# Products of 32 columns behind the first units' stages, and the global normalising step placed behind the next unit's maxima

## The chip, the cores and the metric

The kernel runs on one core of one Trainium2 chip. The metric is the device time of one execution in microseconds. PE is the engine of matrix products (TensorE), with its weight loads shown apart as PEld; DVE is VectorE, ACT is ScalarE, POOL is GpSimd, and SP (SyncE) issues the DMAs.

## The reference

The reference computes attention over 8 batches of 8 heads with 512 local and 32 global positions, head dimension 64, and then a gated feed-forward network on the result. A global query attends to all 544 keys. A local query attends to the 32 global keys and to the local keys at a distance of at most 32.

```python
k_all = np.concatenate([k_g, k_l], axis=2)
v_all = np.concatenate([v_g, v_l], axis=2)
out_g = sm(scale * q_g @ k_all.T) @ v_all            # sm: softmax over the keys, + 1e-9 in the sum
s_ll  = np.where(abs(i - j) <= 32, scale * q_l @ k_l.T, -1e9)
out_l = sm(concat([scale * q_l @ k_g.T, s_ll])) @ v_all
x     = concat([out_g, out_l])   # 4608 tokens of 512
gate  = 1 / (1 + exp(-(x @ w_gate)))                 # 512 x 1536
out   = (gate * (x @ w_val)) @ w_out                 # 1536 x 512
```

All is in 32-bit floats.

## The kernel before, in words

**Two streams in one.** The feed-forward network (`ffn_stream`) is the backbone of the program. It goes through the tokens in chunks: the two halves of batch 0 (256 tokens each), batches 1 to 7 (512 each), and at the end all global tokens. For each chunk it goes through 12 tiles of 128 of the 1536 inner columns. Each step is 12 products of the gate (PSUM tile `bank_g`, L400), 12 of the value (`bank_v`, L400) and 12 of the output of the step before (`bank_o`, L437). Each operand is split into a high and a low part and the product is made of three passes over them, which is why there are 12 products for 4 slices of the contraction.

After every 4 products the stream yields, and a clock `now` goes on by one slot. A batch of 512 tokens thus has 12 x 9 = 108 slots. The attention of the next chunk is cut into events with due times on this clock (`att_events`), and after each yield all events that are due are written into the program.

**A unit of attention** (`local_unit`) takes two blocks of 128 queries of one head through four stages, due 0, 3, 6 and 9 slots after the unit's start (`STAGES`). Units start 4 slots apart.

- Stage 0: scores on PE (L234, into `bank_x`), then for each block the masked maxima on VectorE (L248, into `nm`, with the scores copied to `s_sb`) and the exponentials on ScalarE (L251).
- Stage 1: sum and reciprocal (L254, L255) and the normalising products (L260, into `p_buf`), on VectorE.
- Stage 2: transposes on PE (L268), a copy on ScalarE and, for the high and low split, a subtraction on VectorE (L279, L280, into `pt`).
- Stage 3: products with the values on PE (L300, into `bank_x`), a copy on ScalarE (L302), a sum on VectorE (L303) and one on POOL (L304).

**The global group.** After the two units of a head its 32 global queries are scored (L313 to L318) and copied into a quarter of `pg_buf` (L320, L321). After the 4th and the 8th head, the group of four heads goes through `global_group`: maxima (L328) and exponentials (L330); the normalising step on VectorE (L335, 128 x 544); five transposes on PE (L340) with their copies (L344) and low parts (L346, into `ptg`); and 20 products (L361). Its stages are due at 0, 3, 6 and 9 slots (`GSTAGES`). After the first group of a batch, the next unit starts 4 slots after the group; after the second group the next unit belongs to the next chunk. There are 16 groups, three of them "native": in the first chunks, operands are taken as plain floats without a split.

**PSUM.** `bank_g`, `bank_v`, and all `bank_x` and `bank_y` tiles share four buffers (tag `att`). The four `bank_o` accumulators have the rest.

**What sets the order.** Each engine works through its own queue in order. The order in a queue is made by a planner when the program is built: it goes by readiness in its own reckoning of durations, and of what is ready takes first what was written first. `with tc.issue_after(ins)` adds an edge: what is issued inside on the engine of `ins` comes behind `ins` in that engine's queue. Three anchors are kept for this: `anchor[0]` is the last L248 that was written, `exp_at[0]` the last L251, `low_at[0]` the last L280.

**The filling products.** `fill(n)` multiplies the identity by itself into a PSUM bank that nobody reads (L117). Eight calls come before the first unit. In the first chunk (8 units, `first`) one call follows the scores, one the transposes and one the products of each unit: 24 calls. The products wait for nothing but the identity.

Of the kernel before, what the change touches and what calls it, by code (L numbers as in the profile page):

```python
# [17 lines left out]
P = 128  # L18
D = 64
SL = 512  # L20
SG = 32
# [22 lines left out]

BASE, PER = 3, 4
STAGES = (0, 3, 6, 9)
GSTAGES = (0, 3, 6, 9)
LOAD_QK, LOAD_V, SPLIT_QK, SPLIT_V = 16, 9, 10, 4
LOAD_V_NATIVE = 4

# [2 lines left out]
FILL = (8, 1)  # L53
# [12 lines left out]
def kernel(ctx, tc, qk, v, w_gate, w_val, w_out, out_l, out_g):  # L66
    nc = tc.nc
# [15 lines left out]
    ident = const.tile([P, P], F32, name="ident")  # L83
# [4 lines left out]
    for c0, nc0, lo, hi in ((0, 128, 0, 64), (160, 64, 128, -64)):  # L88
        cols = mid[:, c0:c0 + nc0]
# [22 lines left out]

    fill_ps = ps.tile([P, DM], F32, name="bank_o3")

    def fill(n):
        for i in range(n):
            nc.tensor.matmul(fill_ps[:, 0:P], ident, ident, start=True, stop=True)  # L117

    fill(FILL[0])
    conv_bufs = []  # L120
    anchor, exp_at, low_at = [None], [None], [None]
# [102 lines left out]
    def local_unit(T, blocks, x32s, h, b0):  # L224
        ks, k0s, q0 = T["qk"], T["k0"], T["q0"]
        nat = T["native"]
# [6 lines left out]
                js = slice(k0 + j * BLK + w0, k0 + j * BLK + w1)  # L233
                nc.tensor.matmul(s_ps[:, i, w0:w1], qj, kt[:, js], start=t == 0, stop=t == last)  # L234
        if T["first"]:
            fill(FILL[1])
        if T["first"]:
            s_sb = ffn.tile([P, 2, WIN], F32, name="s_first", tag="ob", bufs=2)
        else:
# [27 lines left out]
        for t, (_, c) in enumerate(tiles):  # L267
            nc.tensor.transpose(pt_ps[:, t], pb[:, c:c + P], ident)  # L268
        if T["first"]:
            fill(FILL[1])  # L270
        if nat:
            if T["first"] and h % 2:
                pt = ffn.tile([P, 4, P], F32, name="pt_first", tag="th", bufs=1)[:, 0:nt]
# [14 lines left out]
        if nat:  # L288
            o_ps = ps.tile([64, 2, P], F32, name="bank_x", tag="att", bufs=4)
            for i, j in enumerate(blocks):  # L290
                for n, tl in enumerate(KEYS[j]):
                    nc.tensor.matmul(o_ps[:, i], vt[:, tl, :], pt[:, at[tl]], start=n == 0, stop=n == 1)  # L292
            if T["first"]:
                fill(FILL[1])
            nc.scalar.copy(dst, o_ps)
            return
        o_ps = ps.tile([P, 2, 2, P], F32, name="bank_x", tag="att", bufs=4)
# [25 lines left out]
    def global_group(Ts, b, g):  # L323

        nat = Ts[0]["native"]
        mg = small.tile([P, 4], F32, name="mg")
        p = pg[:, G0:G0 + KALL]
        nc.vector.tensor_reduce(mg[:, 0:1], p, axis=AX.X, op=ALU.max)  # L328
        nc.vector.tensor_scalar(mg[:, 1:2], mg[:, 0:1], -0.125, None, op0=ALU.mult)
        nc.scalar.activation(p, p, AF.Exp, bias=mg[:, 1:2], scale=0.125, accum_out=mg[:, 2:3])  # L330
        nc.vector.tensor_scalar_add(mg[:, 3:4], mg[:, 2:3], 1e-9)
        nc.vector.reciprocal(mg[:, 3:4], mg[:, 3:4])
        yield
        with tc.issue_after(low_at[0].ins) if not nat else nullcontext():
            nc.vector.tensor_scalar(p, p, mg[:, 3:4], None, op0=ALU.mult)  # L335
        yield
        banks = [ps.tile([P, n, GH, SG], F32, name="bank_y", tag="att", bufs=4) for n in (4, 1)]
        for j in range(5):
            o = banks[j // 4][:, j % 4].rearrange("p r q -> p (r q)")
            nc.tensor.transpose(o, pg[:, j * P:(j + 1) * P], ident)  # L340
        pt = att.tile([P, 5, GH, 2, SG], F32 if nat else F32R, name="ptg_nat" if nat else "ptg", tag="ptg", bufs=1)
        for bank, t in zip(banks, (pt[:, 0:4], pt[:, 4:5])):
            hi, lo = t[:, :, :, 0], t[:, :, :, 1]
            nc.scalar.copy(hi, bank)  # L344
            if not nat:
                nc.vector.tensor_tensor(lo, bank, hi.bitcast(F32), op=ALU.subtract)  # L346
        yield
        g0 = b * SG
        xg = xgq[g0 // P][g0 % P:g0 % P + SG, g * GH * D:(g + 1) * GH * D].rearrange("q (r d) -> q r d", d=D)
        if nat:  # L350
            o_ps = ps.tile([SG, GH, D], F32, name="bank_x", tag="att", bufs=4)
            for r, T in enumerate(Ts):
                for j in range(5):
                    nc.tensor.matmul(o_ps[:, r], pt[:, j, r, 0], T["v"][:, V_GLOBAL[j], :], start=j == 0,
                                     stop=j == 4)
            nc.scalar.copy(xg, o_ps)
            return
        o_ps = ps.tile([2 * SG, GH, 2 * D], F32, name="bank_x", tag="att", bufs=4)
        for r, T in enumerate(Ts):
            for j in range(5):  # L360
                nc.tensor.matmul(o_ps[:, r], pt[:, j, r].rearrange("p c q -> p (c q)"), T["v"][:, V_GLOBAL[j], :],  # L361
                                 start=j == 0, stop=j == 4)
        y = att.tile([SG, GH, 2 * D], F32, name="yq", tag="t0", bufs=1)
        nc.scalar.copy(y, o_ps[SG:2 * SG])
        nc.vector.tensor_tensor(y, o_ps[0:SG], y, op=ALU.add)
        nc.gpsimd.tensor_tensor(xg, y[:, :, 0:D], y[:, :, D:2 * D], op=ALU.add)
# [82 lines left out]
    def att_events(ci, start, per, tail=0):  # L449
# [21 lines left out]
        def adv(h, i):  # L471
            if (h, i) not in gens:
                gens[h, i] = (local_unit(heads[h], units[i], x32s, h, blocks[0]) if i < nu
                              else global_group(heads[h + 1 - GH:h + 1], b, h // GH))
            next(gens[h, i], None)

        npu = nu + (1 if with_g else 0)
        for h in range(NH):
# [7 lines left out]
            for i in range(npu):  # L486
                t0 = base + per * i
                if i == nu:
                    ev.append((t0, 2, lambda T=T, h=h: global_scores(T, h % GH)))
                    if h % GH < GH - 1:  # L490
                        continue
                for o in STAGES if i < nu else GSTAGES:
                    ev.append((t0 + sc * o, 2, lambda h=h, i=i: adv(h, i)))
# [122 lines left out]
```

## Time and profile before

| what | value |
|---|---|
| median of 3 runs | 1168.41 us (1167.89 to 1168.96) |
| the profiled execution | 1169.24 us |
| its span, first to last instruction | 1167.2 us |
| PE busy | 1142.7 us, 98% |
| ScalarE busy | 748.2 us, 64% |
| VectorE busy | 723.9 us, 62% |
| POOL busy | 365.4 us, 31% |
| mean granted TensorE clock | 1.000 |

A row of the profile gives a line of the kernel, an engine, an operation with its tiles, a count, the busy time, the mean duration of one in nanoseconds, and the idle time of the engine before it with what ended it. A row of the timeline begins with the start in microseconds from the span's start and the duration. Ends of PE's products are modelled, and products overlap in the pipeline, so a busy PE is not PE at its peak. A row of the stretches gives busy time and number of instructions for PE, PEld, DVE, ACT and POOL, then the granted clock, the share of the DMA engines and GB/s.

### The profile page before, as it was taken

To read this page: it belongs to the slowest core of one execution; us is meant where nothing else is said; L and a number is where in the kernel's file an instruction comes from. 1 tells how busy PE (TensorE), PEld (TensorE's weight loads), DVE (VectorE), ACT (ScalarE), POOL (GpSimd) and SP (SyncE) were. 2 spreads that over 40 slices of the span, in tenths; PEclk is the share of its full clock that TensorE was granted. 3 is DMA by queue.
4 is the path that set the end of the run, shared out by engine and by line. 5 is a ranking of instruction groups with operands and counts; after the bars stand their busy time and mean duration, and the time that the engine had idled before them with its cause. 6 is when DMAs were issued, how large, how long until landed. Compare 5 with 4: busy or idle time off the path is not lost.

```text
span 1167.2 us, 18885 instructions
## 1 busy us (share of the span) xinstructions
PE 1142.7 (98%) x6596; PEld 958.7 (82%) x6596; DVE 723.9 (62%) x1950; ACT 748.2 (64%) x1700; POOL 365.4 (31%) x372
## 2 busy tenths in 40 slices
PE   8999999999999999999999999999999999999998
PEld 7777888888888888888888888887888888888897
DVE  5888746566676666656676666666666666533343
ACT  5888767666676676666676676677675676432343
POOL 1000135234452444334452444344442443100000
PEclk9999999999999999999999999999999999999999
DMA  8898744343333333443343333353243332122143
GB/s 299 289 297 295 237 135 129 96 123 101 104 117 119 106 112 99 109 143 100 102 117 119 108 110 99 109 151 109 84 127 121 109 106 75 55 90 72 55 157 115
DMA packets 59486, 151.79 MB, mean 130 GB/s; under 512 B 6144, under 2 KB 19456, under 8 KB 59392
## 3 DMA queue, kind: packets, MB, share of 16 engines
q1 hardware_dynamic: 59392, 150.59, 42.6%
q8 instruction: 52, 0.85, 0.3%
q14 instruction: 42, 0.34, 0.1%
HBM read 135.36 MB, written 15.20 MB: 129 GB/s over the span
## 4 chain that ended last, share of the span: by engine, by line
PE 74%; ACT 11%; DVE 10%; issue 2%; DMA 1%; POOL 1%; SPq 0%; DVEq 0%; ACTq 0%
PE bank_g L400 19%; PE bank_o L437 19%; PE bank_v L400 18%; PE bank_x L234 4%; PE bank_y L268 3%; PE bank_x L300 3%; ACT s_sb L251 3%; PE bank_x L292 2%; DVE p_buf L260 2%; DVE pt L280 1%; PE bank_x L361 1%; DVE bank_v L421 1%; DVE t L303 1%; DVE bank_v L420 1%; ACT mn L414 1%
## 5 line engine op out<-in xcount | busy, mean ns | idle before, releaser
L400 PE MATMUL bank_v<-xt,wv 128*128 128x512 f32 (+1 forms) x1440 | 328.2, 364 | 6.8 <-DVE t L303 6.8
L400 PE MATMUL bank_g<-xt,wg 128*128 128x512 f32 (+1 forms) x1440 | 329.7, 364 | 0.2 <-DVE t L303 0.2
L437 PE MATMUL bank_o<-wo,hh 128*128 128x512 f32 x1224 | 325.6, 398 | 0.6 <-ACT hh L423 0.6
L400 PEld LDWEIGHTS bank_v<-xt,wv 128*128 128x128 f32 x1440 | 237.2, 189 | 43.7 <-DVE t L303 8.3
L400 PEld LDWEIGHTS bank_g<-xt,wg 128*128 128x128 f32 x1440 | 236.9, 189 | 37.1 <-issue 2.9
L437 PEld LDWEIGHTS bank_o<-wo,hh 128*128 128x128 f32 x1224 | 217.1, 188 | 40.5 <-ACT hh L423 1.4
L251 ACT ACTIVATE s_sb<-s_sb,nm 128x192 f32<-128x192 f32 (+1 forms) x240 | 110.7, 462 | 92.0 <-DVE nm L248 91.7
L205 POOL TENSOR_TENSOR kl<-qk_raw,qk_hi 128x704 fp32r<-128x704 f32 x52 | 88.6, 1704 | 156.8 <-ACT qk_hi L204 151.6
L423 ACT CAST hh<-bank_v 128x512 fp32r<-128x512 f32 (+1 forms) x120 | 62.7, 522 | 109.9 <-DVE bank_v L421 109.1
L218 POOL TENSOR_TENSOR vhl<-v_raw,vhl 128x512 fp32r<-128x512 f32 x52 | 67.3, 1294 | 186.5 <-ACT vhl L217 85.4
L303 DVE TENSOR_TENSOR t<-bank_x,t 64x512 f32<-64x512 f32 x104 | 70.8, 681 | 86.5 <-ACT t L302 85.4
L408 ACT ACTIVATE th<-bank_g 128x512 f32<-128x512 f32 (+1 forms) x120 | 63.9, 532 | 90.4 <-PE bank_g L400 89.8
L304 POOL TENSOR_TENSOR x<-t 64x256 f32<-64x256 f32 x104 | 76.9, 740 | 124.0 <-DVE t L303 101.2
L413 DVE TENSOR_SCALAR mn<-bank_g 128x512 f32<-128x512 f32 (+1 forms) x108 | 67.7, 627 | 76.8 <-ACT th L408 76.7
L248 DVE CUSTOM_DVE_ANT_0 s_sb<-bank_x,masks 128x192 f32<-128x192 f32 (+1 forms) x240 | 80.8, 370 | 30.7 <-PE bank_x L234 27.1
L420 DVE TENSOR_TENSOR bank_v<-bank_v,mn 128x512 f32<-128x512 f32 (+1 forms) x120 | 73.7, 614 | 42.1 <-PE bank_v L400 36.8
L424 DVE TENSOR_TENSOR hh<-bank_v,hh 128x512 fp32r<-128x512 f32 (+1 forms) x120 | 73.2, 610 | 41.0 <-ACT hh L423 40.2
L373 POOL TENSOR_TENSOR xt<-x,xt 128x512 fp32r<-128x512 f32 (+1 forms) x36 | 42.7, 1187 | 152.7 <-ACT xt L372 108.2
L280 DVE TENSOR_TENSOR pt<-bank_y,pt 128x384 fp32r<-128x384 f32 x104 | 64.6, 621 | 37.7 <-ACT pt L279 37.0
L260 DVE TENSOR_SCALAR p_buf<-s_sb,r 128x192 f32<-128x192 f32 (+1 forms) x240 | 83.0, 374 | 2.0
L207 POOL TENSOR_TENSOR qk_hi<-qk_raw,qk_hi 64x256 fp32r<-64x256 f32 x104 | 78.6, 776 | 4.1
L300 PEld LDWEIGHTS bank_x<-pt,vhl 128*128 128x128 f32 x416 | 61.6, 189 | 18.7 <-issue 7.5
(108 smaller groups left out, 1577.1 us busy)
## 6 DMA issues: line engine op xcount, KB each, us to landing
wo<-wo_dram SPq DMA_DIRECT2D x116, 512.0 KB, 3.5
qk_raw<-in_qk_dram SPq DMA_DIRECT2D x104, 312.0 KB, 4.4
v_raw<-in_v_dram SPq DMA_DIRECT2D x52, 256.0 KB, 2.6
out_dram<-ob SPq DMA_DIRECT2D x34, 256.0 KB, 2.9
xt<-in_w_gate_dram SPq DMA_DIRECT2D x12, 512.0 KB, 6.1
xt<-in_w_val_dram SPq DMA_DIRECT2D x12, 512.0 KB, 6.2
xt<-in_w_out_dram SPq DMA_DIRECT2D x12, 512.0 KB, 5.9
v_nat<-in_v_dram SPq DMA_DIRECT2D x8, 512.0 KB, 6.5
```

The costliest lines, as they stand in the source:

```text
L205: nc.gpsimd.tensor_tensor(kl, t[:, K0:Q1], hi[:, K0:Q1].bitcast(F32), op=ALU.subtract)
L207: nc.gpsimd.tensor_tensor(hi[64:128, r], t[64:128, r], hi[64:128, r].bitcast(F32), op=ALU.subtract)
L248: anchor[0] = nc.vector.tensor_tensor_reduce(out=s_sb[:, i, w], in0=s_ps[:, i, w], in1=mid[:, w], scale=-0.125, scalar=3.0e38, op0=ALU.add ...
L251: exp_at[0] = nc.scalar.activation(s_sb[:, i, w], s_sb[:, i, w], AF.Exp, bias=nm[:, i:i + 1], scale=-1.0, accum_out=sm[:, i:i + 1])
L260: nc.vector.tensor_scalar(pb[:, places[i] + w0:places[i] + w1], s_sb[:, i, w0:w1], r[:, i:i + 1], None, op0=ALU.mult)
L280: low_at[0] = nc.vector.tensor_tensor(pt[:, 1], pt_ps, pt[:, 0].bitcast(F32), op=ALU.subtract)
L300: nc.tensor.matmul(o_ps[:, i], vt[:, tl, :], pt[:, :, at[tl], :], start=n == 0, stop=n == 1)
L303: nc.vector.tensor_tensor(t0, o_ps[0:64], t0, op=ALU.add)
L304: nc.gpsimd.tensor_tensor(dst, t0[:, :, 0], t0[:, :, 1], op=ALU.add)
L400: nc.tensor.matmul(acc, w[a][:, t, fs], xt[:, c, t, x0:x0 + ntok], start=n == 0, stop=n == 11)
L420: nc.vector.tensor_tensor(acc, acc, mn, op=ALU.mult)
L437: nc.tensor.matmul(o_ps[t], ph[:, a, t * P:(t + 1) * P], pwo[:, c], start=f2 == 0 and i == 0, stop=f2 == NF - 1 and i == 2)
```

## The change

The 24 calls of `fill` behind the stages of the first units multiply the identity by its first 32 columns instead of all 128; the eight calls ahead of them stay. The global group's second stage (the normalising step L335) is due 5 slots after its start instead of 3, the third (transposes) 7 instead of 6. In the groups that are not native, the step's edge goes to the last maxima written, `anchor[0]`, instead of the last low part of a transposed unit, `low_at[0]`. As the next unit's stage 0 is due 4 slots after a first group's start, its two L248 are written by then.

```diff
-GSTAGES = (0, 3, 6, 9)
+GSTAGES = (0, 5, 7, 9)
...
-    def fill(n):
+    def fill(n, cols=P):
         for i in range(n):
-            nc.tensor.matmul(fill_ps[:, 0:P], ident, ident, start=True, stop=True)
+            nc.tensor.matmul(fill_ps[:, 0:cols], ident, ident[:, 0:cols], start=True, stop=True)
...
         if T["first"]:
-            fill(FILL[1])
+            fill(FILL[1], SG)
...
         if T["first"]:
-            fill(FILL[1])
+            fill(FILL[1], SG)
...
             if T["first"]:
-                fill(FILL[1])
+                fill(FILL[1], SG)
...
-        with tc.issue_after(low_at[0].ins) if not nat else nullcontext():
+        with tc.issue_after(anchor[0].ins) if not nat else nullcontext():
             nc.vector.tensor_scalar(p, p, mg[:, 3:4], None, op0=ALU.mult)
```

## The prediction

> **What bounds the kernel now.** I read the page first: busy shares and the chain that ended last.
>
> ```profile
> span 1167.2 us, 18885 instructions
> PE 1142.7 (98%) x6596; PEld 958.7 (82%) x6596; DVE 723.9 (62%) x1950; ACT 748.2 (64%) x1700; POOL 365.4 (31%) x372
> PE 74%; ACT 11%; DVE 10%; issue 2%; DMA 1%; POOL 1%; SPq 0%; DVEq 0%; ACTq 0%
> ```
>
> PE sets the end: 98% busy and 74% of the chain. A change can win in two ways only: by taking work from PE, or by taking away a wait of PE. So the waits of PE come next, for the part of the span in which one batch is like the other (280 to 1000 us).
>
> ```profile
> PE bank_v L400 <- DVE t L303: 6.8, 6, 1.1
> ```
>
> This is by far the largest of them: 6.8 us in six instances, the longest 1.1 us. Its place is seen in the timeline of one instance, PE first, then VectorE, then ScalarE, and last the same wait one batch earlier.
>
> ```profile
> 419.04 0.27 PE L234 MATMUL bank_x<-kl,qk_hi 128*128 128x192 f32 x1
> 420.10 0.64 PE L300 MATMUL bank_x<-pt,vhl 128*128 128x256 f32 x4
> 421.50 0.71 PE L340 MATMUL bank_y<-ident,pg_buf 128*128 128x128 f32 x5
> 423.35 0.50 PE L400 MATMUL bank_v<-xt,wv 128*128 128x512 f32 x1 [1.15 <-DVE t L303]
> ...
> 419.00 0.69 DVE L280 TENSOR_TENSOR pt<-bank_y,pt 128x512 fp32r<-128x512 f32 x1
> 419.61 1.05 DVE L335 TENSOR_SCALAR pg_buf<-pg_buf,mg 128x544 f32<-128x544 f32 x1
> 420.57 0.34 DVE L248 CUSTOM_DVE_ANT_0 s_sb<-bank_x,masks 128x192 f32<-128x192 f32 x1
> 420.85 0.35 DVE L248 CUSTOM_DVE_ANT_0 s_sb<-bank_x,masks 128x192 f32<-128x192 f32 x1
> 421.98 0.17 DVE L254 TENSOR_SCALAR r<-sm 128x2 f32<-128x2 f32 x1 [0.78 <-ACT s_sb L251]
> 422.39 0.32 DVE L260 TENSOR_SCALAR p_buf<-s_sb,r 128x192 f32<-128x192 f32 x1
> 422.62 0.68 DVE L303 TENSOR_TENSOR t<-bank_x,t 64x512 f32<-64x512 f32 x1
> ...
> 420.96 0.46 ACT L251 ACTIVATE s_sb<-s_sb,nm 128x192 f32<-128x192 f32 x1 [2.00 <-DVE nm L248]
> 421.98 0.58 ACT L302 COPY t<-bank_x 64x512 f32<-64x512 f32 x1
> ...
> 292.84 0.96 PE L400 MATMUL bank_v<-xt,wv 128*128 128x512 f32 x3 [1.13 <-DVE t L303]
> ```
>
> To be seen: the scores of the next unit are done at 419.31 (419.04 + 0.27). Their maxima (L248) start only at 420.57, because VectorE is in the global normalising step L335 from 419.61 on. ScalarE, idle for 2.00 us, starts the exponentials at 420.96, its copy L302 stands behind them at 421.98, the sum L303 ends at 423.30, and 0.05 us later bank_v has a PSUM buffer. The step that the change moves is the head of the wait. The two waits end 130.51 us apart, one batch; a slot of the written order is 130.51 / 108 = 1.21 us.
>
> **The change part by part.** *The edge.* At the first global group of a batch the last maxima before the step's new place are those of the next unit, so L335 goes behind both L248. Nothing is added or removed; the step issues no DMA and no POOL work, and on VectorE it is moved past the two L248 alone. From the rows above: L280 ends at 419.69, the scores are there at 419.31, so the first L248 starts at about 419.6, 0.97 us earlier. Both take 420.85 + 0.35 - 420.57 = 0.63 us, so L335 runs from 420.23 to 421.28. The exponentials move forward by 0.97 too, and L302 to 421.01 (its input L300 is done at 420.74, so that is no limit), ending at 421.59. L303 then depends on VectorE's order. Straight after L302 it ends near 422.33: 0.97 saved. Behind L254, L255 and L260, as now, it starts where the first L260 is nearly over: these begin at 421.28 behind L335 instead of 421.98, so L303 ends at 422.60, 0.70 saved. I take the middle, 0.83, and six instances: 5.0 us. Bounds: nothing (below), and the whole wait, 6.8 us. What is late next: L335 ends at 421.28 and the transposes L340 begin at 421.50, so 0.22 us of slack remains for them.
>
> *The two slots moved.* The step goes from slot 3 to 5, its transposes (five of PE, two copies L344, two subtractions L346) from 6 to 7, the products L361 stay at 9. Work is the same; what can change is whether L361 finds its input. First the first group, then the second of a batch, whose L303 and L280 also count:
>
> ```profile
> 425.50 0.29 DVE L346 TENSOR_TENSOR ptg<-bank_y,ptg 128x128 fp32r<-128x128 f32 x1 [0.77 <-ACT ptg L344]
> 426.67 1.36 PE L361 MATMUL bank_x<-vhl,ptg 128*64 128x128 f32 x20
> ...
> 477.58 0.17 DVE L332 RECIPROCAL mg<-mg 128x1 f32<-128x1 f32 x1
> 478.00 0.68 DVE L303 TENSOR_TENSOR t<-bank_x,t 64x512 f32<-64x512 f32 x1 [0.25 <-ACT t L302]
> 479.22 1.07 DVE L335 TENSOR_SCALAR pg_buf<-pg_buf,mg 128x544 f32<-128x544 f32 x1
> 484.60 0.28 DVE L346 TENSOR_TENSOR ptg<-bank_y,ptg 128x128 fp32r<-128x128 f32 x1
> 484.88 1.36 PE L361 MATMUL bank_x<-vhl,ptg 128*64 128x128 f32 x20
> ```
>
> The first has 426.67 - 425.79 = 0.88 us of slack, the second none. PE's order is planned anew with the later input, so I take no cost; one slot of delay kept by the products is a rival below. In the second group no unit of its batch follows: the new edge names maxima long done, and L335 may go into VectorE's idle 0.25 us at 477.75, ahead of L303 and L280. That can cost PE up to one L335, 1.07 us, in 7 groups. I take nothing there, since the step now stands behind both in the written order, and keep 7.5 us as a bound. The three native groups never had the edge; their step can shift by one duration: bound 3 us either way.
>
> *The 32 columns.* The products, their weight loads, rows of narrower shapes, and where they lie on the chain:
>
> ```profile
> L117 PEld LDWEIGHTS bank_o<-ident x64: 186/192/333, 5.4 to 29.4; 128*128 128x128 f32 x64
> L117 PE MATMUL bank_o<-ident x64: 275/275/582, 5.4 to 29.5; 128*128 128x128 f32 x64
> L292 PEld LDWEIGHTS bank_x<-pt_nat,v_nat x160: 132/137/137, 13.1 to 160.3; 128*64 128x64 f32 x160
> L354 PE MATMUL bank_x<-v_nat,ptg_nat x120: 219/219/243, 66.4 to 166.8; 128*32 128x64 f32 x120
> 66.45 2.35 PE bank_x L354 x40
> 5.52 6.34 PE bank_o L117 x36
> 21.54 1.09 PE bank_o L117 x8
> 28.49 1.31 PE bank_o L117 x10
> 20.00:30.00 10.00, 10.00 (x67) 7.96 (x67) 8.22 (x32) 8.71 (x25) 0.73 (x1) 1.00 0.93 289
> ```
>
> A call is two PE instructions (32 calls, 64 rows). The first 8 calls keep 128 columns, so 48 rows get 32. At full clock one more costs (1.31 - 1.09) / 2 = 0.11 us. A weight load of 128 columns lasts 192 ns and one of 64 lasts 137: 0.86 ns a column, 0.11 us for 128. The load alone fills the spacing, and it stays: the change cuts the streamed side only. So the price stays 0.11 us, except for the last product of each of the six stretches, which nothing follows: a product of 128 columns lasts 275 ns and one of 64 lasts 219, so 96 columns are 96 x 56 / 64 = 84 ns each, 0.5 us together. Below lies the pace of L354, 2.35 / 40 = 0.059 us, with weights of 32 columns: 48 x (0.11 - 0.059) = 2.4 us gained. Above: the planner may believe in shorter products and put more of them before the first transposes. 36 rows stand there, 28 after; if all 28 went there, the units would start 28 x 0.11 = 3.1 us later, and as ScalarE and VectorE are 87% and 82% busy in the ten microseconds from 20 on, little of it might come back. I take 0.5 us gained, from -2.4 to +3.1.
>
> Here a rule speaks against the change. These products also keep the array's clock up, as two equal-shaped stretches show:
>
> ```profile
> 6.46 3.41 PE L117 MATMUL bank_o<-ident 128*128 128x128 f32 x15
> 10.02 1.61 PE L117 MATMUL bank_o<-ident 128*128 128x128 f32 x13
> ```
>
> 0.23 us each (3.41 / 15), then 0.12 (1.61 / 13): the array ran at half pace until about 10 us, 4.5 us after the first of them. If shorter products delayed that once more by as much, 4.5 us at half pace would lose 2.2 us. By the Trainium skill (TensorE: Matmul & The Clock Gate, section "The HAM clock gate") the array starts at half rate and gets full rate only after a window of sustained activity; an array idle for three quarters of each product might not pass, and by this rule the sum would lose its gain from the fills and 2.2 us more. The trace agrees on the two paces, but no row shows how narrow products count; I weigh it as part of a rival.
>
> **The sum.** The profiled execution took 1169.24 us, 2.04 around its span, and lies 0.83 above the median of the runs, 1168.41. 1169.24 - 5.0 - 0.5 = 1163.7; less 0.83 is **1162.9 us**, 0.47% faster.
>
> **The rivals.**
> *B, another cover goes.* L340, 0.71 us, now stands between bank_g and bank_v and covers part of the wait. If its later slot puts it behind bank_v, PE reaches bank_v 0.71 us sooner while L303 comes 0.70 sooner: the wait stays, and the change doesn't do what it says. For it: the slack of 0.22 us. Against: late transposes would leave two buffers to bank_v. Time: 1168.4 - 0.5 = 1167.9.
> *C, slower: the global products wait.* If the transposed rows come one slot later and PE keeps L361's place, PE waits 1.21 - 0.88 = 0.33 us in 6 first groups and 1.21 in 7 second groups: 10.5 us against 5.5, so 1173.4. It decides from a delay of 0.88 us in the first and of any size in the second groups. For it: the zero slack at 484.88; against: the planner knows of the delay. L335 ahead of L280 in the second groups, 7.5 us, would end near 1170.4.
> *D, the opening gives it back.* All 48 rows before the first transposes (+3.1) or a late full clock (+2.2), with 5.0 won in the batches: between 1166.5 and 1168.7, I take 1167. For it: ScalarE and VectorE leave little room; against: PE's total falls, not rises.
>
> **How the numbers follow.** My forecast 0.58 (its own range 1159 to 1166: 6.8 + 2.4 gained, or six times 0.70 with some of the opening lost), B 0.17, C 0.14, D 0.11. Below 0.2% (2.3 us) this measurement can't tell a change from none. Faster: 0.57 from the forecast, 0.04 from the near ends of B and D: 0.61. Slower: 0.14 from C and 0.03 from native groups or a D with both costs: 0.17. Same: 0.22. For 8 in 10 the range goes from 1159.5, nearly the forecast's lower end, to 1170.5, which takes in B, D and the early end of C.
>
> **What would show it.** In each batch L248 starts about 0.6 us after the end of the scores' last product or less, and L335 behind it; the 1.1 us of bank_v on L303 shrink to 0.45 or less. L117's 48 rows keep 0.11 us spacing; a spacing near 0.06 would prove the weight-load argument wrong. The first transposes (now 11.7 us) tell whether rows were moved up. The prediction is wrong if PE waits at L361, L340 or L300 for VectorE by as much as bank_v lost, or if the opening ends over 2 us later than now.

## The result, and the profile after

The changed kernel takes 1178.86 us (median of 4 runs, 1175.55 to 1181.01), the kernel before took 1168.15 beside it. The ratio is 1.0084, with a 95% interval of 1.0071 to 1.0096: slower, and above the stated range of 1159.5 to 1170.5, where a gain of 0.5% was forecast. The mean granted clock was 1.000 before; in the four runs after it is 0.991, 0.996, 0.994 and 0.996. The profiled execution took 1180.11 us.

The page of the changed kernel:

```profile
span 1178.0 us, 18866 instructions
PE 1153.9 (98%) x6596; PEld 963.8 (82%) x6596; DVE 718.5 (61%) x1950; ACT 748.8 (64%) x1700; POOL 365.3 (31%) x372
PE 66%; ACT 14%; DVE 13%; issue 3%; DMA 2%; POOL 2%; DVEq 0%; SPq 0%; ACTq 0%
```

PE does the same 6596 products and is busy for 11.2 us more. **Where the time went** is seen in the timeline of PE in the opening, first before, then after:

```profile
11.70 0.60 PE L268 MATMUL bank_y<-ident,p_buf 128*128 128x128 f32 x4
35.80 0.62 PE L400 MATMUL bank_g<-xt,wg 128*128 128x256 f32 x3
```

```profile
5.43 10.75 PE L117 MATMUL bank_o<-ident 128*128 128x128 f32 x64
15.99 0.45 PE L268 MATMUL bank_y<-ident,p_buf 128*128 128x128 f32 x1
...
19.18 1.97 PE L292 MATMUL bank_x<-pt_nat,v_nat 128*64 128x128 f32 x8
...
32.53 1.09 PE L292 MATMUL bank_x<-pt_first,v_nat 128*64 128x128 f32 x8
...
45.38 0.62 PE L400 MATMUL bank_g<-xt,wg 128*128 128x256 f32 x3
```

All 64 filling products now stand ahead of the first transposes, which start 4.3 us later, and the feed-forward stream starts 9.6 us later. The same eight products L292 take 1.97 us at 19 us and 1.09 at 32.5. The stretches of the changed kernel say why; the column behind POOL is the granted clock (it is recorded from its first grant on, at 8.0 us here, so an earlier 1.00 would be no reading):

```profile
8.10:11.40 3.30, 3.30 (x33) 3.30 (x31) 0.79 (x4) 0.00 (x0) 0.00 (x0) 1.00 1.06 402
11.50:31.90 20.40, 20.40 (x77) 15.79 (x77) 6.28 (x27) 7.65 (x22) 0.73 (x1) 0.50 0.47 172
32.00:45.00 13.00, 9.66 (x66) 7.19 (x65) 10.63 (x37) 11.59 (x32) 1.46 (x2) 1.00 0.89 267
```

The clock was granted, taken back to half near 11.4 us in the middle of the narrow products, and given again only near 31.9 us: 20.5 us at half, with PE never idle in them.

**The batches.** The largest of the waits of PE from 290 to 1010 us, and the first group of the batch that the prediction followed, PE and then VectorE:

```profile
PE bank_x L361 <- DVE ptg L346: 3.9, 15, 0.3
```

```profile
429.46 0.27 PE L234 MATMUL bank_x<-kl,qk_hi 128*128 128x192 f32 x1
...
431.91 1.09 PE L400 MATMUL bank_v<-xt,wv 128*128 128x512 f32 x4
432.84 0.71 PE L340 MATMUL bank_y<-ident,pg_buf 128*128 128x128 f32 x5
...
436.00 1.41 PE L361 MATMUL bank_x<-vhl,ptg 128*64 128x128 f32 x20 [0.15 <-DVE ptg L346]
```

```profile
430.01 0.35 DVE L248 CUSTOM_DVE_ANT_0 s_sb<-bank_x,masks 128x192 f32<-128x192 f32 x1
430.29 0.35 DVE L248 CUSTOM_DVE_ANT_0 s_sb<-bank_x,masks 128x192 f32<-128x192 f32 x1
430.56 0.50 DVE L335 TENSOR_SCALAR pg_buf<-pg_buf,mg 128x544 f32<-128x544 f32 x1
...
432.07 0.68 DVE L303 TENSOR_TENSOR t<-bank_x,t 64x512 f32<-64x512 f32 x1
```

The 6.8 us of bank_v waiting for L303 are gone. L335 stands behind both L248, and bank_v starts without a wait at 431.91, ahead of L340, 0.16 us before L303 has even begun. In its place L361 waits, 3.9 us in 15 instances. Most of that lies in the second groups; PE before, then PE and VectorE after:

```profile
478.35 2.00 PE L400 MATMUL bank_v<-xt,wv 128*128 128x512 f32 x8
...
481.59 0.71 PE L340 MATMUL bank_y<-ident,pg_buf 128*128 128x128 f32 x5
...
488.85 2.88 PE L400 MATMUL bank_v<-xt,wv 128*128 128x512 f32 x12
```

```profile
487.73 2.00 PE L400 MATMUL bank_v<-xt,wv 128*128 128x512 f32 x8
...
491.88 0.71 PE L340 MATMUL bank_y<-ident,pg_buf 128*128 128x128 f32 x5
...
494.70 0.45 PE L361 MATMUL bank_x<-vhl,ptg 128*64 128x128 f32 x4 [0.27 <-DVE ptg L346]
495.50 1.17 PE L361 MATMUL bank_x<-vhl,ptg 128*64 128x128 f32 x16 [0.34 <-DVE ptg L346]
...
499.30 2.88 PE L400 MATMUL bank_v<-xt,wv 128*128 128x512 f32 x12
```

```profile
487.15 0.93 DVE L335 TENSOR_SCALAR pg_buf<-pg_buf,mg 128x544 f32<-128x544 f32 x1
488.00 0.68 DVE L303 TENSOR_TENSOR t<-bank_x,t 64x512 f32<-64x512 f32 x1
...
493.96 0.69 DVE L346 TENSOR_TENSOR ptg<-bank_y,ptg 128x512 fp32r<-128x512 f32 x1 [0.76 <-ACT ptg L344]
494.56 0.68 DVE L424 TENSOR_TENSOR hh<-bank_v,hh 128x512 fp32r<-128x512 f32 x1
495.16 0.28 DVE L346 TENSOR_TENSOR ptg<-bank_y,ptg 128x128 fp32r<-128x128 f32 x1
```

The same work from one bank_v to the next takes 11.57 us instead of 10.50: 1.07 us lost. The transposes stand one block of output products later (3.24 us behind the first bank_v before, 4.15 after), and the second low part L346 stands behind L424 on VectorE. The first groups win about as much. From the gate products ahead of the scores to the next unit's transposes the stretch was 417.81 to 428.83 before and 428.23 to 438.21 after, 11.02 and 9.98 us. If all groups are like these two, 6 x 1.04 = 6.2 us are won and 7 x 1.07 = 7.5 lost.

### The profile page after: what moved, and what is told of

Its sections match the earlier page's. It is cut to its first block, busy times and chain, and to the rows that moved or that the text cites. A ratio compares the mean times of both kernels' runs of the same rounds, so it can differ in the third digit from the quotient of the medians.

```text
span 1178.0 us, 18866 instructions
## 1 busy us (share of the span) xinstructions
PE 1153.9 (98%) x6596; PEld 963.8 (82%) x6596; DVE 718.5 (61%) x1950; ACT 748.8 (64%) x1700; POOL 365.3 (31%) x372
## 4 chain that ended last, share of the span: by engine, by line
PE 66%; ACT 14%; DVE 13%; issue 3%; DMA 2%; POOL 2%; DVEq 0%; SPq 0%; ACTq 0%
PE bank_g L400 17%; PE bank_o L437 17%; PE bank_v L400 15%; PE bank_x L234 4%; PE bank_y L268 3%; ACT s_sb L251 3%; PE bank_x L300 3%; DVE t L303 2%; DVE p_buf L260 2%; DVE pt L280 2%; PE bank_x L292 2%; ACT mn L414 2%; PE bank_x L361 1%; ACT qk_hi L204 1%; DVE bank_v L421 1%
## 5 line engine op out<-in xcount | busy, mean ns | idle before, releaser
L437 PEld LDWEIGHTS bank_o<-wo,hh 128*128 128x128 f32 x1224 | 217.2, 188 | 40.7 <-ACT hh L423 1.4
L303 DVE TENSOR_TENSOR t<-bank_x,t 64x512 f32<-64x512 f32 x104 | 70.8, 680 | 82.0 <-ACT t L302 80.9
L304 POOL TENSOR_TENSOR x<-t 64x256 f32<-64x256 f32 x104 | 76.3, 733 | 116.3 <-DVE t L303 93.4
L248 DVE CUSTOM_DVE_ANT_0 s_sb<-bank_x,masks 128x192 f32<-128x192 f32 (+1 forms) x240 | 80.7, 370 | 28.4 <-PE bank_x L234 24.6
L424 DVE TENSOR_TENSOR hh<-bank_v,hh 128x512 fp32r<-128x512 f32 (+1 forms) x120 | 73.1, 609 | 38.3 <-ACT hh L423 37.5
L280 DVE TENSOR_TENSOR pt<-bank_y,pt 128x384 fp32r<-128x384 f32 x104 | 64.4, 620 | 37.1 <-ACT pt L279 36.4
```

The source lines that it names most:

```text
L248: anchor[0] = nc.vector.tensor_tensor_reduce(out=s_sb[:, i, w], in0=s_ps[:, i, w], in1=mid[:, w], scale=-0.125, scalar=3.0e38, op0=ALU.add ...
L280: low_at[0] = nc.vector.tensor_tensor(pt[:, 1], pt_ps, pt[:, 0].bitcast(F32), op=ALU.subtract)
L303: nc.vector.tensor_tensor(t0, o_ps[0:64], t0, op=ALU.add)
L304: nc.gpsimd.tensor_tensor(dst, t0[:, :, 0], t0[:, :, 1], op=ALU.add)
L437: nc.tensor.matmul(o_ps[t], ph[:, a, t * P:(t + 1) * P], pwo[:, c], start=f2 == 0 and i == 0, stop=f2 == NF - 1 and i == 2)
```

## The experiments

The theory after the result: the opening loses to the clock, because narrow products behind full weight loads hardly count as activity; the batches win in the first groups and lose in the second. All runs:

| run | median us, kernel before beside it | ratio, 95% interval |
|---|---|---|
| e1, 32 columns alone | 1174.61, 1168.36 | 1.0051 (1.0035 to 1.0068) |
| e2, global step alone | 1170.99, 1168.36 | 1.0017 (1.0007 to 1.0026) |
| e3, step in the first groups alone | 1162.76, 1168.36 | 0.9948 (0.9932 to 0.9963) |
| e4, all fills ahead, 128 columns | 1170.74, 1168.36 | 1.0016 (1.0005 to 1.0027) |
| e5, 64 columns | 1168.71, 1167.80 | 1.0012 (1.0003 to 1.0021) |
| e6, no fills behind the units | 1168.04, 1167.80 | 1.0003 (0.9992 to 1.0013) |
| e7, slots 5 and 7 in all groups, old edge in the second | 1170.80, 1167.80 | 1.0027 (1.0017 to 1.0037) |
| e8, as e3, first products one slot later | 1162.49, 1167.80 | 0.9952 (0.9938 to 0.9967) |
| e9, as e3, no fills behind the units | 1160.62, 1168.36 | 0.9948 (0.9933 to 0.9963) |
| e10, 48 columns | 1170.48, 1168.36 | 1.0034 (1.0014 to 1.0055) |

### The two halves apart

```diff
 # e1: the changed kernel with
-GSTAGES = (0, 5, 7, 9)
+GSTAGES = (0, 3, 6, 9)
-        with tc.issue_after(anchor[0].ins) if not nat else nullcontext():
+        with tc.issue_after(low_at[0].ins) if not nat else nullcontext():
 # e2: the kernel before with these two lines the other way round
```

> The 32 columns alone; the global step stands as before. Theory: the whole loss is in the opening. All 24 narrow calls stand ahead of the first transposes, the clock is taken back to half while they run, and the feed-forward stream starts near 45 us instead of 35.8; the batches repeat as before with the 1.15 us wait of bank_v. Time 1168.2 + 9.6, 1176 to 1179. Rival (the step delays the stream as well, and the opening costs only what 28 more rows ahead of the transposes cost): 1168.2 + 3, 1170 to 1172.

> The global step alone; the fills keep 128 columns. Theory: in each batch the first group wins about 1.04 us (11.02 to 9.98 us from the gate products to the next unit's transposes) and the second loses about 1.07 (10.50 to 11.57 us from its value products to the next ones), as L361 waits for L346. With 6 first and 7 second groups: 1168.2 - 6.2 + 7.5 = 1169.5, within 1168 to 1170.5. The prediction's theory (first groups win, second cost nothing): 1163. The clock stays at full from about 10 us on.

The stretches of e1, and the start of its stream:

```profile
11.10:14.40 3.30, 3.30 (x28) 3.02 (x27) 0.00 (x0) 0.00 (x0) 0.00 (x0) 1.00 1.05 402
14.50:24.60 10.10, 10.10 (x36) 7.36 (x36) 3.49 (x17) 4.46 (x14) 0.00 (x0) 0.50 0.50 174
24.70:40.00 15.30, 11.59 (x76) 8.43 (x75) 13.08 (x46) 14.07 (x39) 2.19 (x3) 1.00 0.76 241
```

```profile
40.97 0.63 PE L400 MATMUL bank_g<-xt,wg 128*128 128x256 f32 x3
```

The clock falls here too, later and for 10.2 us instead of 20.5, and the stream starts 5.2 us late. The cost, 6.2 us, is smaller than I expected (9.6) and larger than the rival's 3. Most of it goes with the half clock: by e4 below, the place of the fills alone delays the stream by 1.65 of the 5.2 us. e2 costs 2.6 us where I expected 1.3 and the prediction's theory had a gain: the two sides of the batches do cancel, and a little more.

The two add up to 8.9 of the 10.7 us. In the opening the changed kernel and e1 have the same order on PE; their profiles differ in when the half clock begins and how long it lasts. The runs point to this for the missing 1.8 us. Of the changed kernel's four runs, the two with a mean clock as in e1's runs (0.996; e1 has 0.995 and 0.996) took 1175.55 and 1177.62 us, on both sides of 1168.15 + 8.9 = 1177.05; the two with less clock (0.991 and 0.994) took 1180.11 and 1181.01.

### The gain without the loss

```diff
-GSTAGES = (0, 3, 6, 9)
+GSTAGES = ((0, 5, 7, 9), (0, 3, 6, 9))
...
-                for o in STAGES if i < nu else GSTAGES:
+                for o in STAGES if i < nu else GSTAGES[h // GH]:
...
-        with tc.issue_after(low_at[0].ins) if not nat else nullcontext():
+        with tc.issue_after((low_at if g else anchor)[0].ins) if not nat else nullcontext():
```

> The new slots and the new edge for the first group of each batch only; the second groups keep slots 3 and 6 and the edge to the last low part; the fills keep 128 columns. Theory (gain of the first groups and loss of the second are independent): 1168.2 - 6.2 = 1162, 1161 to 1163. Rival (the gain of the first groups is given back somewhere else in the batch whatever the second groups do): within 1 us of 1168.

1162.76 us, as expected: 5.6 us faster. The waits from 280 to 1000 us are two rows now:

```profile
PE bank_x L300 <- DVE mn L413: 1.1, 6, 0.2
PE bank_x L361 <- DVE ptg L346: 1.1, 6, 0.2
```

So the gain of the first groups is real and does not depend on the change in the second. Whether the new edge or the new slots bring it is open: e3 changes both in the first groups, and no run parts them there. Which of the two edits costs the second groups their 1.07 us, e7 says: it gives them slots 5 and 7 and leaves them the old edge.

```diff
-GSTAGES = ((0, 5, 7, 9), (0, 3, 6, 9))
+GSTAGES = ((0, 5, 7, 9), (0, 5, 7, 9))
```

> New slots 5 and 7 for both groups, but the second groups keep their edge to the last low part; fills with 128 columns. It parts the two edits of the second groups. Theory (the transposes one slot later are what makes L361 wait): as with the whole step, 1169.5 to 1171, with the waits of L361 for L346 near 4.9 us in 17 instances. Rival (the step L335 ahead of L303 and L280, which the new edge allows, is what costs): 1162 to 1163.5.

1170.80 us, with L361 waiting for L346 from 280 to 1000 us:

```profile
PE bank_x L361 <- DVE ptg L346: 6.1, 16, 0.7
```

It is the slots, and the waits are somewhat longer than expected (6.9 us in 18 instances over the whole span). The new edge does let L335 go ahead of L303 and L280 in the second groups (in the changed kernel's second group above it starts at 487.15 us, L303 at 488.00), and that costs nothing that can be seen: e2, with the new edge, is no slower than e7.

In e8 the first groups' products stand one slot later, to take away their 1.1 us.

```diff
-GSTAGES = ((0, 5, 7, 9), (0, 3, 6, 9))
+GSTAGES = ((0, 5, 7, 10), (0, 3, 6, 9))
```

> First groups new as in the run with the first groups alone, and their products L361 one slot later (10 instead of 9); second groups as before; fills with 128 columns. Theory (the 1.1 us of L361 waiting for L346 in the first groups is a real wait): 1162.8 - 1.1 = 1161.7. Rival (the later products hold their PSUM buffer later and a wait of the same size stands elsewhere): 1162.8.

1162.49 us, not to be told from e3. The rival holds: the wait only moved, to the PSUM buffer of the later products (280 to 1000 us).

```profile
PE bank_g L400 <- DVE yq L365: 2.0, 6, 0.7
```

### Width or place

e4 has the place of the changed kernel's fills without their narrowness.

```diff
-FILL = (8, 1)
+FILL = (32, 0)
```

> All 32 fill calls ahead of the first transposes with 128 columns each, none between the units; the global step as before. It has the place of the changed kernel's fills without their width. If the width takes the clock away (narrow products hardly count as activity): full clock is granted near 8 to 10 us and stays while the fills run, to about 14.8 us; the units behind them are slower or not by whether they hold the clock alone. If they do hold it: 1168.2 + 0 to 2. If the place is what matters (units without fills between them don't hold the clock): the clock falls after 15 us and the time is near 1175 or more.

Its stretches, and two rows of its PE timeline:

```profile
11.50:15.90 4.40, 4.40 (x39) 4.23 (x39) 0.00 (x0) 0.38 (x1) 0.00 (x0) 1.00 1.05 403
16.00:31.90 15.90, 13.62 (x88) 9.98 (x87) 13.15 (x53) 13.65 (x42) 1.46 (x2) 1.00 0.75 243
32.00:45.00 13.00, 10.77 (x62) 8.12 (x61) 9.94 (x27) 9.95 (x26) 1.67 (x2) 0.87 0.85 277
```

```profile
14.88 0.60 PE L268 MATMUL bank_y<-ident,p_buf 128*128 128x128 f32 x4
...
37.45 0.62 PE L400 MATMUL bank_g<-xt,wg 128*128 128x256 f32 x3
```

The clock stays at full while 128 columns stream, and also behind them, in the 15.9 us of the second row, in which only the units' own products run. The transposes start 3.2 us late, as in the prediction's count, and of that 1.65 us reach the stream. So of the 9.6 us by which the stream of the changed kernel starts late, the place accounts for 1.65; the other 7.9 go with the lost clock, and this is net of a first grant that came 2.0 us earlier there (8.03 against 10.00 us).

Two things do not fit the theory as neatly. The median, 1170.74 us, is 2.4 above that of before, a little over the 0 to 2 expected. And this execution does lose the clock later, in the stream: for one step of 3.4 us from 40.7 us on, which is the 0.87 of the third row. No narrow product runs there, so narrow products are not the only way to lose the clock; what caused this fall was not followed.

Then the width alone, in two steps, 64 columns (e5) and 48 (e10), in the kernel of e1, at each of the three calls:

```diff
-            fill(FILL[1], SG)
+            fill(FILL[1], 2 * SG)          # e5
+            fill(FILL[1], SG + SG // 2)    # e10
```

> The fills behind the units' stages get 64 columns instead of 32, the global step as before. One size changed: the array streams for half of each product instead of a quarter; the weight loads keep the spacing at 0.112 us, and 18 of the 24 calls stand ahead of the first transposes. If the clock is taken away by how little the array streams, 64 columns either pass (full clock throughout, stream start near 37.5 us, about 1169 to 1171) or fail as 32 did (half clock for some windows of 3.41 us, 1174 or more); either answer bounds the share that counts as activity. If narrowness has no part in it, half clock comes here as often as with 32 columns and the time is 1174 to 1176 again.

> The fills behind the units' stages get 48 columns, the global step as before. 23 of the 24 calls stand ahead of the first transposes, almost as with 32 columns, where all 24 do: the place is the same, the width alone differs. Theory (the width decides): either the clock is held in all runs (1168 to 1170.5, the share that passes lies below 48 / 128) or lost as with 32 columns (1174 to 1176). Rival (the number of rows ahead of the transposes decides): lost, 1174 to 1176, like 32 columns and unlike 64, where 18 calls stood ahead.

| columns | calls ahead of the transposes | runs that lost the clock, by their mean | mean granted clock |
|---|---|---|---|
| 32 (changed kernel, e1) | 24 | 8 of 8 | 0.991 to 0.996 |
| 48 (e10) | 23 | 3 of 10 | 0.991 to 0.994, else 1.000 |
| 64 (e5) | 18 | 0 of 10 | 0.999 to 1.000 |

The three runs of e10 that lost it took 1176.3, 1177.3 and 1181.2 us, the other seven 1168.3 to 1171.0. With 23 of 24 calls at the same place, 48 columns pass in most executions and 32 in none: the width decides, and 48 of 128 lies on the border. I had expected all or none. The three widths ran on three chips, so a part of the difference could be the chips'; e4, with 128 columns, ran on the same chip as e1.

The traces also say why the same narrow products lose the clock sooner in one execution than in another. Counting the columns of the products that begin in each step of 3.41 us at full clock, the changed kernel streamed 1376 in its first step (4 products of 128 columns and 27 of 32) and lost the clock at its end. e1, granted 0.4 us earlier, streamed 1696 in its first step (7 and 25), kept the clock, streamed 1248 in the second and lost it. e10 kept it with 1968 and 1776. This holds for these runs of fills in five steps, and is no rule for other work.

The stretch in which e1 was at half clock, in the profile of e10, which kept it:

```profile
14.30:24.50 10.20, 9.64 (x63) 7.14 (x61) 7.00 (x32) 7.75 (x23) 0.73 (x1) 1.00 0.67 235
```

Last, no fills behind the units at all (e6), and with them left out the step of e3 (e9). The 24 calls compute nothing that is read.

```diff
-FILL = (8, 1)
+FILL = (8, 0)
```

> The eight wide calls stay ahead, the 24 behind the units' stages are left out (they compute nothing that is read); the global step as before. Theory (units hold or win the clock themselves, narrow products are worse than none): transposes start near 9 us, full clock is granted by the window that ends near 10 to 13.5 us, the stream starts near 34 to 36 us, time 1167 to 1169, well below the 1174.6 of the narrow fills. Rival (without filling products the units alone don't win the clock): half clock for several windows, as in the changed kernel from 16 to 32 us, and 1174 or more.

> The first groups' new slots and edge (second groups as before) together with the eight wide fills alone, the 24 behind the units left out. Theory (the two gains are of different places, opening and batches): the stream starts near 32 us and the batches last 129.6 us; 1162.8 less what of the earlier start arrives at the batches, 0 to 2.1 us: 1160.7 to 1162.8. Rival (the earlier start moves every later wait, as the two long batches of the run without the unit fills hint): not below 1162.8.

e6 takes 1168.04 us: no products are better than narrow ones by about 6 us, and equal to the wide ones. Two of its ten runs have a clock of 0.997 and take 1170.8 and 1170.9, so the units alone hold it in most executions, not in all. e9 has the lowest median, 1160.62 us, but its ratio of 0.9948 is that of e3. Its opening:

```profile
5.40 2.77 PE L117 MATMUL bank_o<-ident 128*128 128x128 f32 x16
...
31.21 0.62 PE L400 MATMUL bank_g<-xt,wg 128*128 128x256 f32 x3
```

The stream starts 4.6 us earlier than before (3.8 in e6, where the clock was granted later, at 8.8 us against 7.0), and the median is 2.1 us below e3's. Where the rest of the earlier start goes was not followed, and two of its six runs lost some clock (0.997, 1163.9 and 1165.3). So the 5.6 us of e3 are shown, and a further gain of e9 is not.

## Why the prediction was wrong

**The wait and its head: right in what moves, in part lucky in the size.** As worked out, L248 starts 0.28 us after the scores' end (430.01 - 429.73) instead of 1.26, L303 comes 0.97 us sooner behind them (2.34 us instead of 3.31), and the wait of bank_v is gone. The forecast of 5.0 us (0.83 a batch) was measured as 5.6 us in e3, 1.04 in the stretch of one batch. But the way there was another: I had L340 stay ahead of bank_v and a rest of 0.18 to 0.45 us. In fact bank_v went ahead of L340, as rival B had it, but without B's price, and started before L303 began, so the earlier L303 is not what let it start. That later transposes leave a buffer to bank_v, B's own counter-argument, fits this order. The earlier L303 (it ends at 432.75, and L340 starts at 432.84) may still be what L340 needs; no run shows how the 5.6 us divide.

**The slots: wrong.** "PE's order is planned anew with the later input, so I take no cost" is the first step that failed. Rival C named the place, the zero slack at L361 in the second groups, and its price there, 1.21 us each; measured were 1.07 us in the stretch. In the first groups C's 0.33 us is 0.15 to 0.2 of recorded wait and is inside the net gain. So the gain of the forecast and the loss of C both came true, in different groups, and cancelled. I had treated them as alternatives.

**The new edge in the second groups: right to take nothing**, with the order feared (L335 ahead of L303 and L280) in place. A loss of the size of its bound did come, 7 x 1.07 = 7.5 us, but e7 shows that it came from the slots.

**The price of a narrow product: right.** The rows of L117 in the changed kernel, first the whole, then, nearly all of 32 columns, a run of them at full clock and one at half:

```profile
L117 PEld LDWEIGHTS bank_o<-ident x64: 192/306/333, 5.4 to 15.7; 128*128 128x128 f32 x64
L117 PE MATMUL bank_o<-ident x64: 195/367/580, 5.4 to 15.8; 128*128 128x32 f32 x48, 128*128 128x128 f32 x16
```

```profile
8.43 3.10 PE L117 MATMUL bank_o<-ident 128*128 128x128 f32 x27
11.36 4.60 PE L117 MATMUL bank_o<-ident 128*128 128x32 f32 x21
```

A product of 32 columns takes 3.10 / 27 = 0.115 us and 4.60 / 21 = 0.22, tails included, as one of 128 did. A quarter of the columns leaves the spacing as it was, which is what the prediction's reading has: the weight load sets the pace.

**The opening: wrong, and this is the larger part.** The failed steps are "I take 0.5 us gained, from -2.4 to +3.1" and rival D's 2.2 us for the clock. D's first half came true: all 48 rows went ahead, and in e4 this alone puts the transposes 3.2 us later at full clock, of which 1.65 us reach the stream. Its second half was mis-sized and misread. I priced a grant that comes 4.5 us later. The grant came earlier than before (8.0 us against about 10); what happened is that the clock was taken back during the narrow products and stayed at half for 20.5 us, more than 15 of them behind the fills, with the units' own products alone. That the products behind the units keep the clock up, as the prediction has it, is not borne out either: without them (e6) eight of ten runs kept it. The term is 7.9 us in place of 2.2, and the range, which had no room for it, missed. Of the signs that the prediction names for its being wrong, the opening is the plain one: it ends 9.6 us later. The rule that the prediction weighed, of the Trainium skill (TensorE: Matmul & The Clock Gate, section "The HAM clock gate"), has an idle window of about 3.4 us put the array back to half rate. The trace agrees on the steps (8.03 to 11.44 us at full is 3.41 us, the 20.48 us at half are six of them) and shows more than the rule says: PE was busy all through the window that lost the clock, and 27 of the 31 products that began in it only streamed a quarter of the columns.

## What to carry to other kernels

To keep the clock up, a filling product had to stream here: with 128 columns of weights loaded for each, in rows of 18 to 24 calls, 32 streamed columns lost the clock in 8 of 8 runs, 48 in 3 of 10 and 64 in none of 10, and each took the same 0.11 us at full clock as one of 128. Leaving the fillers out was as fast as the wide ones. A filler that nothing waits for can be moved by its width alone: here 10 calls stood ahead of the transposes with 128 columns, 18 with 64 and all 24 with 32, so a "cheaper" filler can end up all in one place. And a step moved within a repeated pattern has to be costed at each kind of place where it repeats: here the first group of a batch had something to overtake, the second only something to delay.

## What the runs showed of the hardware

The normalising step L335 lasts 0.50 us behind the maxima and 1.05 where it stood before (the groups' rows at 430.56 and, in the prediction, at 419.61), for the same 128 x 544 elements:

```profile
L335 DVE TENSOR_SCALAR pg_buf<-pg_buf,mg x16: 497/504/925, 74.2 to 1011.2; 128x544 f32<-128x544 f32 x16
```

What sets the longer times can be read from POOL's rows. In the traces of before and after, 22 of the 32 instances of L335 last 0.58 to 1.07 us, and each of them ends 0.30 us after the end of the POOL instruction that runs when it starts or begins within 0.05 us of that: POOL ends 0.28, 0.62 or 0.77 us after the start of L335, and L335 lasts 0.58, 0.92 or 1.07. The ten that last 0.50 us have no such instruction beside them, or one that ends within 0.20 us. That fits the exclusive port that VectorE, in a mode that uses two ports, and POOL share by the Trainium skill (SBUF — State Buffer, section "SBUF: two separate sides"), where the one that comes second waits for the whole instruction. No row says in which mode L335 ran. So about 0.55 us of the 1.05 at the head of the old wait were POOL's (L304 runs beside L335 there), not the step's own. This was read from the overlaps and not tested by a run.
